# A delta-rule scan before two gated MLPs: the gate made in place in PSUM, second products two steps behind, key operands loaded ahead

## The chip, the cores and the metric

The kernel runs on one core of one Trainium2 chip. The metric is the device time of one execution in microseconds. Of three runs of the kernel before, the median is 1048.21 us (1047.57 to 1048.82).

## The reference

```python
def _attn_ref(q, k, v, beta):
    k_n = k / (norm(k, axis=-1) + 1e-06)
    for t in range(S):
        y[:, :, t] = q[:, :, t] @ state
        v_old = state^T @ k_n[:, :, t]
        state = state + beta[t] * outer(k_n[:, :, t], v[:, :, t] - v_old)
x = y, heads side by side                        # 3072 tokens x 384
h = x @ w_in;  x = (h * sigmoid(1.702 * h)) @ w_out        # first MLP, d_ff 2048
h = max(x @ w_in2, 0);  out = (h * h) @ w_out2             # second MLP, d_ff 2048
```

There are 4 batches, 8 heads, 768 tokens and a head width of 48. All data are float32.

## The kernel before

The scan is cut into 12 chunks of 64 tokens. A chunk `n` goes through `run_a` (keys times keys and keys times queries on PE, copied by ACT into `G` and `pqa`/`pqb`), `solve_in`, `solve_norm`, `solve_prep` and `solve_loop` (a triangular system, on DVE for chunk 0 and on POOL for the others), `finish` and `merge` (transposes and, for chunks 0 to 3, two blocks of 64 small products on PE with an ACT copy into `kT_sb` between them), and then `run_x`, `run_w`, `run_g`, `run_w`, `run_y`, `run_s` (products with the state, whose results are the columns of the MLP's input).

The first MLP (lines 760 to 801, `ph == 1`) takes tiles of 512 tokens, that is two chunks; the second (`ph == 2`) runs after it on the same tiles. One `step` is one of 16 slices of 128 hidden rows. Each float32 operand is split into a high and a low part, so a product is three matmuls (high by high, high by low, low by high). A step puts 9 matmuls of 512 columns into one of two PSUM banks `h`. Then ACT makes tanh (or relu) of the bank into `g`, DVE makes the gated `g` (lines 793 and 796), ACT rounds it into `ghi`, and DVE makes `glo`, the rest. `layer2` adds 9 matmuls with `ghi` and `glo` into three banks `z`. The list `prev` holds steps whose `layer2` is still to come: one for full tiles, two for the half tiles at the start. The first tile is done in halves, since chunk 0 is ready before chunk 1, and while the scan goes on its blocks are put between the steps of the first MLP. The weights are split as they arrive (`split_w`, on ACT, DVE and POOL).

The order on each engine is fixed when the kernel is built. `Program.add` takes an operation with its assumed duration, what it reads and what it writes; `flush` (lines 102 to 187) plays a list schedule with these durations and, on each engine, issues the operation of lowest rank that is ready. On the chip each engine then goes through its list in that order. All DMAs of inputs go out from SP's list.

`load_kq` fetches the operands of `run_a`, four groups of 256 KB for each chunk. From chunk 2 on there are two buffers: groups 0 and 1 are loaded in the scan of two chunks earlier, groups 2 and 3 only behind the products of groups 0 and 1:

```python
put(0, lambda: run_a(m, 0, ((m, 2), (m, 3))))     # line 894
...
mms((1.0, 1.75), todo, reads, [A for _, A in ps_of])   # line 405
for x in nxt:
    load_kq(*x)
```

`run_a` makes, for each pair of groups, 16 products of a 64x64 key block with 128 columns. Only the 32x32 blocks on the diagonal of keys times keys are wanted twice over, so ACT copies each 32-partition strip by itself (lines 412 to 416): two of 256 columns and two of 128 for each group.

## Time and profile before

| | us |
|---|---|
| median of three runs | 1048.21 |
| the profiled execution's own time | 1046.38 |
| its span, first to last instruction | 1044.7 |
| PE busy in the span | 969.3 |
| DVE, ACT, POOL busy | 597.9, 528.4, 336.7 |

PE is TensorE's matmuls, PEld its weight loads, DVE VectorE, ACT ScalarE, POOL GpSimd, SP the queue that issues DMAs. A row of a timeline gives start, duration, engine, line, operation, output and input tiles, count, and in brackets the engine's idle time before it with what ended that. Matmuls overlap in their pipeline, so a single duration is longer than the distance to the next one.

### The profile page before, as it was taken

To read this page: it belongs to the slowest core of one execution; us is meant where nothing else is said; L and a number is where in the kernel's file an instruction comes from. 1 tells how busy PE (TensorE), PEld (TensorE's weight loads), DVE (VectorE), ACT (ScalarE), POOL (GpSimd) and SP (SyncE) were. 2 spreads that over 40 slices of the span, in tenths; PEclk is the share of its full clock that TensorE was granted. 3 is DMA by queue.
4 is the path that set the end of the run, shared out by engine and by line. 5 is a ranking of instruction groups with operands and counts; after the bars stand their busy time and mean duration, and the time that the engine had idled before them with its cause. 6 is when DMAs were issued, how large, how long until landed. Compare 5 with 4: busy or idle time off the path is not lost.

```text
span 1044.7 us, 24071 instructions
## 1 busy us (share of the span) xinstructions
PE 969.3 (93%) x9900; PEld 780.2 (75%) x9900; DVE 597.9 (57%) x1182; ACT 528.4 (51%) x1088; POOL 336.7 (32%) x672
## 2 busy tenths in 40 slices
PE   4479698989888999999999999999999999999998
PEld 3377586767666777777787787788888888888886
DVE  6787786765377576764854667864343333433332
ACT  4566756653655657566535556544343343433333
POOL 2253551288547848748670111210000000000000
PEclk7687888999999999999999999999999999999999
DMA  8254543230322313132111435421010010000000
GB/s 233 85 164 122 168 127 93 65 104 22 96 73 75 97 53 116 43 97 76 55 32 60 137 112 152 121 61 61 1 51 11 0 61 1 21 11 1 31 1 30
DMA packets 43982, 76.33 MB, mean 73 GB/s; under 512 B 6624, under 2 KB 19552, under 8 KB 43872
## 3 DMA queue, kind: packets, MB, share of 16 engines
q1 hardware_dynamic: 43776, 74.75, 23.9%
q8 instruction: 77, 1.26, 0.5%
q14 instruction: 33, 0.27, 0.1%
q10 hardware_dynamic: 96, 0.05, 0.0%
HBM read 64.16 MB, written 9.44 MB: 70 GB/s over the span
## 4 chain that ended last, share of the span: by engine, by line
PE 57%; DVE 16%; POOL 10%; ACT 8%; issue 4%; DMA 3%; SPq 1%; DVEq 0%; ACTq 0%; POOLq 0%
PE z L311 26%; PE h L311 25%; PE a L311 5%; POOL tmpp L567 4%; POOL U L570 4%; ACT G L276 2%; DMA kq<-in_kf 2%; DVE v_sb L286 2%; DVE glo L286 2%; DVE g L293 2%; DVE c L290 1%; DVE c L293 1%; SPq L258 1%; ACT ws L276 1%; ACT ghi L271 1%
## 5 line engine op out<-in xcount | busy, mean ns | idle before, releaser
L271 ACT ACTIVATE g<-h 128x512 f32<-128x512 f32 (+1 forms) x200 | 114.8, 578 | 251.5 <-PE h L311 238.3
L311 PE MATMUL z<-glo,wo_hi 128*128 128x512 f32 (+1 forms) x600 | 232.1, 387 | 8.2 <-DVE glo L286 7.7
L311 PE MATMUL z<-ghi,wo_hi 128*128 128x512 f32 (+1 forms) x600 | 233.4, 389 | 0.1
L311 PE MATMUL z<-ghi,wo_lo 128*128 128x512 f32 (+1 forms) x600 | 230.0, 383 | 0.0
L286 DVE TENSOR_TENSOR glo<-g,ghi 128x512 fp32r<-128x512 f32 (+1 forms) x200 | 140.5, 704 | 100.3 <-ACT ghi L271 98.8
L271 ACT ACTIVATE ghi<-g 128x512 fp32r<-128x512 f32 (+1 forms) x200 | 122.5, 614 | 127.1 <-DVE g L293 64.5
L286 DVE TENSOR_TENSOR g<-g,h 128x512 f32<-128x512 f32 x96 | 66.0, 687 | 157.5 <-ACT g L271 157.5
L311 PE MATMUL h<-x_hi,wi_hi 128*128 128x512 f32 (+1 forms) x312 | 128.1, 411 | 14.4 <-DVE g L293 9.3
L311 PEld LDWEIGHTS z<-glo,wo_hi 128*128 128x128 f32 x600 | 113.8, 190 | 36.7 <-DVE glo L286 15.6
L567 POOL TENSOR_TENSOR tmpp<-U,gu 128x126 f32<-128x126 f32 (+22 forms) x248 | 113.5, 458 | 73.1 <-DVE U L290 54.7
L311 PEld LDWEIGHTS z<-ghi,wo_hi 128*128 128x128 f32 x600 | 113.8, 190 | 23.9 <-ACT ghi L271 0.5
L311 PEld LDWEIGHTS z<-ghi,wo_lo 128*128 128x128 f32 x600 | 113.9, 190 | 21.5
L311 PE MATMUL h<-x_lo,wi_hi 128*128 128x512 f32 (+1 forms) x312 | 120.3, 386 | 0.9 <-DVE x_lo L286 0.8
L311 PE MATMUL h<-x_hi,wi_lo 128*128 128x512 f32 (+1 forms) x312 | 119.5, 383 | 0.0
L570 POOL TENSOR_TENSOR U<-U,tmpp 128x126 f32<-128x126 f32 (+22 forms) x248 | 108.3, 437 | 21.1 <-DVE U L290 2.1
L311 PE MATMUL h<-x_hi,vi_hi 128*128 128x512 f32 x288 | 112.3, 390 | 0.0
L311 PE MATMUL h<-x_hi,vi_lo 128*128 128x512 f32 x288 | 112.1, 389 | 0.0
L293 DVE SCALAR_TENSOR_TENSOR g<-g,h 128x512 f32<-128x512 f32 (+1 forms) x104 | 66.1, 641 | 68.8 <-ACT g L271 68.3
L311 PEld LDWEIGHTS h<-x_hi,wi_hi 128*128 128x128 f32 x312 | 61.0, 195 | 35.5 <-DVE g L293 15.5
L311 PEld LDWEIGHTS h<-x_hi,wi_lo 128*128 128x128 f32 x312 | 61.3, 197 | 11.0
L311 PEld LDWEIGHTS h<-x_lo,wi_hi 128*128 128x128 f32 x312 | 61.4, 197 | 10.0 <-DVE x_lo L286 1.4
L286 POOL TENSOR_TENSOR wo_lo<-c,wo_hi 128x384 fp32r<-128x384 f32 x21 | 22.6, 1075 | 132.4 <-ACT wo_hi L271 132.4
(119 smaller groups left out, 1365.1 us busy)
## 6 DMA issues: line engine op xcount, KB each, us to landing
...
kq<-in_kf SPq DMA_DIRECT2D x44, 256.0 KB, 3.9
...
xf_sb<-zd SPq DMA_DIRECT2D x18, 256.0 KB, 2.7
out<-zs SPq DMA_DIRECT2D x18, 256.0 KB, 2.0
```

The source lines that it names most:

```text
L258: pg.add(queue, 0.07, lambda e: e.dma_start(out=dst, in_=src), reads, writes, early, nbytes)
L271: pg.add("act", c_act(n), lambda e: e.activation(**kw), reads, writes, early)
L276: e.activation(out=out, in_=in_, func=AF.Copy)
L286: pg.add(queue, cost, lambda e: e.tensor_tensor(out=out, in0=in0, in1=in1, op=op), reads, writes, early)
L290: pg.add("dve", c_dve(n, True), lambda e: e.tensor_scalar(**kw), reads, writes, early)
L293: pg.add("dve", c_dve(n), lambda e: e.scalar_tensor_tensor(**kw), reads, writes, early)
L311: e.matmul(out=out, lhsT=lhsT, rhs=rhs, start=start, stop=stop)
L567: e.tensor_tensor(out=t, in0=U[:, lo:hi, j:j + 1].to_broadcast(shape), in1=gu[:, j + 1:, j:j + 1].rearrange("p i o -> p o i").to_broadcast ...
L570: e.tensor_tensor(out=U[:, lo:hi, j + 1:], in0=U[:, lo:hi, j + 1:], in1=t, op=ALU.add)
```

## The change

- `step` writes the gated value over its own `h` bank: DVE's output, ACT's input for `ghi` and DVE's input for `glo` are all that bank. `g` is one buffer of 512 columns in place of two and holds only the tanh or relu. `ghi` and `glo` have three buffers each.
- `layer2` runs two steps behind for all tiles, and what is left is done at the end.
- All four groups of `load_kq` have a buffer from chunk 2 on, and all four are loaded in the scan of two chunks earlier.
- `run_a` makes its products in blocks of 64 rows by 32 columns and puts the second diagonal block where one copy of 128 partitions by 256 columns takes all of `G` of a group. The lower strips skip what is not used, but for chunks 0 and 1, whose banks were never written.
- The buffers `xs` and `tmpd` are gone: `Td` and the second `gu` take their place, so chunk 0's solve on DVE also counts as a writer of the second `gu`.
- Nearly all assumed durations, latencies and DMA rates of the planner have new values, so the order moves on every engine.

```diff
-    LATENCY, OWN_LATENCY = 0.2, 0.12
-    TICK, WARM_COLUMNS = 3.41, 3060
-    DMA_START, DMA_END, DMA_RATE = 1.2, 1.0, 330e3
+    LATENCY, OWN_LATENCY = 0.13, 0.12
+    TICK, WARM_COLUMNS = 3.413, 2950
+    DMA_START, DMA_END, DMA_RATE = 1.6, 0.8, 300e3
...
-    NG = 2
-    g_sb = several(main, "g", NG, [128, TT])
+    NG = 3
+    g_sb = main.tile([128, TT], F32, name="g_sb")
...
-    xs_sb = att.tile([128, CT], F32, name="xs_sb")
+    xs_of = [t.rearrange("p a t -> p (a t)")[:, 0:CT] for t in Td_sb]
...
-        pg.add(queue, 0.07, lambda e: e.dma_start(out=dst, in_=src), reads, writes, early, nbytes)
+        pg.add(queue, 0.62 if nbytes < 40000 else 0.42, lambda e: e.dma_start(out=dst, in_=src), reads, writes, early, nbytes)
...
-            t, keys = kq_sb[g % 2], [("kq", g % 2)]
+            t, keys = (kq_sb, kq1_sb)[g // 2][g % 2], [(("kq", "kq1")[g // 2], g % 2)]
...
-                    o = r if e else 64 - r
-                    todo.append((ps_of[e][0][o:o + 64, 128 * p:128 * p + 128], tiles[e][r:r + 64, 0, p, :], tiles[e][r:r + 64, :, p, :], True, True))
-        mms((1.0, 1.75), todo, reads, [A for _, A in ps_of])
-        for x in nxt:
-            load_kq(*x)
+                    o, t = r if e else 64 - r, tiles[e][r:r + 64, :, p, :]
+                    out = ps_of[e][0][:, 128 * p:128 * p + 128]
+                    todo.append((out[o:o + 32], t[:, 0, 0:32], t, True, True))
+                    low = out[o + 32:o + 64].rearrange("p (c t) -> p c t", c=4)
+                    todo.append((low[:, ::3], t[:, 0, 32:64], t[:, :, 32:64], True, True))
+                    if n < 2:
+                        todo.append((low[:, 1:3], t[:, 0, 32:64], t[:, :, 0:32], True, True))
+        mms((1.25, 2.1), todo, reads, [A for _, A in ps_of])
...
-            for r in range(0, 128, 32):
-                if r % 64 == 0:
-                    copy(256, [A], [("G", i, g + e, r)], G[r:r + 32, sl, :], v4[r:r + 32, :, 0, :])
-                else:
-                    copy(128, [A], [("G", i, g + e, r)], G[r:r + 32, sl, 0:32], v4[r:r + 32, :, 0, 32:64])
+            copy(256, [A], [("G", i, g + e, r) for r in range(0, 128, 32)], G[:, sl, :], v4[:, :, 0, :])
...
-            pg.add(queue, cost, fn, gu_keys(n) + [("U", n % 2)], [("U", n % 2)] + (["first"] if n == 0 and j == 14 else []))
+            pg.add(queue, cost, fn, gu_keys(n) + [("U", n % 2)], [("U", n % 2)] + (gu_keys(1) if queue == "dve" else []) + (["first"] if n == 0 and j == 14 else []))
...
-        g, hi, lo = (x[s][:, o:o + n] for x in (g_sb, ghi_sb, glo_sb))
-        kg, khi, klo = ([(x, s, i) for i in parts] for x in ("g", "ghi", "glo"))
+        g, hi, lo = g_sb[:, o:o + n], ghi_sb[s][:, o:o + n], glo_sb[s][:, o:o + n]
+        kg = [("g", i) for i in parts]
+        khi, klo = ([(x, s, i) for i in parts] for x in ("ghi", "glo"))
         if ph == 1:
             act(n, [("h", p)], kg, out=g, in_=ps, func=AF.Tanh, scale=GATE / 2)
-            stt(n, [("h", p)] + kg, kg, out=g, in0=g, scalar=1.0, in1=ps, op0=ALU.add, op1=ALU.mult)
+            stt(n, [("h", p)] + kg, [("h", p)], out=ps, in0=g, scalar=1.0, in1=ps, op0=ALU.add, op1=ALU.mult)
         else:
             act(n, [("h", p)], kg, out=g, in_=ps, func=AF.Relu)
-            tt(n, [("h", p)] + kg, kg, g, g, ps, ALU.mult)
-        act(n, kg, khi, out=hi, in_=g)
-        tt(n, kg + khi, klo, lo, g, hi, ALU.subtract)
+            tt(n, [("h", p)] + kg, [("h", p)], ps, g, ps, ALU.mult)
+        act(n, [("h", p)], khi, out=hi, in_=ps)
+        tt(n, [("h", p)] + khi, klo, lo, ps, hi, ALU.subtract)
         prev.append((ph, j, f, c0, n, hi, lo, khi + klo))
-        while len(prev) > (1 if n == TT else TUNE["depth"]):
+        while len(prev) > TUNE["depth"]:
             layer2(*prev.pop(0))
...
-                put(4, lambda: load_kq(m + 2, 0), lambda: load_kq(m + 2, 1), lambda: load_q(m + 2))
+                put(4, *[lambda g=g: load_kq(m + 2, g) for g in range(4)], lambda: load_q(m + 2))
...
-            put(0, lambda: run_a(m, 0, ((m, 2), (m, 3))))
+            put(0, lambda: run_a(m, 0))
...
-        layer2(*prev.pop(0))
+        while prev:
+            layer2(*prev.pop(0))
```

The order at three places follows. The first is ACT at chunk 0's merge: the copy that the second block of the merge waits for is `kT_sb<-a_72`. Before:

```order
L276 ACTIVATE G_106<-z_69 32x4x32
L276 ACTIVATE G_106<-z_69 32x256
L276 ACTIVATE G_106<-z_69 32x4x32
L276 ACTIVATE G_106<-z_70 32x256
L276 ACTIVATE G_106<-z_70 32x4x32
L276 ACTIVATE G_106<-z_70 32x256
L276 ACTIVATE G_106<-z_70 32x4x32
L276 ACTIVATE G_106<-z_71 32x256
L276 ACTIVATE G_106<-z_71 32x4x32
L276 ACTIVATE G_106<-z_71 32x256
L276 ACTIVATE G_106<-z_71 32x4x32
L276 ACTIVATE kT_sb<-a_72 128x256
```

With the change:

```order
L277 ACTIVATE G_107<-a_74 128x256
L277 ACTIVATE G_107<-z_69 128x256
L272 ACTIVATE wi_hi<-c_93 128x384
L272 ACTIVATE c_92<-raw_90 128x384
L277 ACTIVATE G_107<-z_70 128x256
L277 ACTIVATE G_107<-z_71 128x256
L277 ACTIVATE pqa_103<-a_74 64x256
L277 ACTIVATE kT_sb<-a_72 128x256
L272 ACTIVATE wo_hi<-c_94 128x384
L272 ACTIVATE c_92<-raw_91 128x384
```

The 16 narrow copies of `G` for chunk 1 (12 of them below `z`, four of another bank ahead of these rows) become four, one weight split stands between them, and the copy into `kT_sb` follows after one copy of `pqa`.

The second is PE in the second MLP. Here `h_67` and `h_68` are the two banks of the step, `z_69` to `z_71` the three output banks. Before:

```order
L311 MATMUL h_68<-x_hi_80,vi_hi 128x512
L311 MATMUL h_68<-x_lo_81,vi_hi 128x512
L311 MATMUL h_68<-x_hi_80,vi_lo 128x512
L311 MATMUL h_67<-x_hi_80,vi_hi 128x512
L311 MATMUL h_67<-x_lo_81,vi_hi 128x512
L311 MATMUL h_67<-x_hi_80,vi_lo 128x512
L311 MATMUL h_68<-x_hi_80,vi_hi 128x512
L311 MATMUL h_68<-x_lo_81,vi_hi 128x512
L311 MATMUL h_68<-x_hi_80,vi_lo 128x512
L311 MATMUL z_69<-ghi_84,wo_hi 128x512
L311 MATMUL z_69<-glo_86,wo_hi 128x512
L311 MATMUL z_69<-ghi_84,wo_lo 128x512
```

With the change:

```order
L313 MATMUL h_68<-x_hi_80,vi_hi 128x512
L313 MATMUL h_68<-x_lo_81,vi_hi 128x512
L313 MATMUL h_68<-x_hi_80,vi_lo 128x512
L313 MATMUL z_69<-ghi_84,wo_hi 128x512
L313 MATMUL z_69<-glo_87,wo_hi 128x512
L313 MATMUL z_69<-ghi_84,wo_lo 128x512
L313 MATMUL h_68<-x_hi_80,vi_hi 128x512
L313 MATMUL h_68<-x_lo_81,vi_hi 128x512
L313 MATMUL h_68<-x_hi_80,vi_lo 128x512
L313 MATMUL z_70<-ghi_84,wo_hi 128x512
L313 MATMUL z_70<-glo_87,wo_hi 128x512
L313 MATMUL z_70<-ghi_84,wo_lo 128x512
```

Before, nine matmuls of `h` are followed by nine of `z`; now they alternate in threes, and so it goes on for the rest of the second MLP.

The third is SP behind chunk 1's output, where the operands for chunk 3 are loaded (`raw` is weights). Before:

```order
L258 DMA k_sb<-in_kt 128x768
L258 DMA raw_89<-in_w_out 128x768
L258 DMA kq_99<-in_kf 128x512
L258 DMA kq_100<-in_kf 128x512
L258 DMA raw_90<-in_w_in 128x768
L258 DMA raw_88<-in_w_out 128x768
L258 DMA kq_99<-in_kf 128x512
L258 DMA kq_100<-in_kf 128x512
L258 DMA raw_89<-in_w_in 128x768
L258 DMA raw_90<-in_w_out 128x768
L258 DMA raw_88<-in_w_in 128x768
L258 DMA kT_sb<-in_kq 128x4x256
```

With the change:

```order
L259 DMA xf_sb<-Td_113 16x256 x6
L259 DMA pqa_103<-in_kq 64x4x256
L259 DMA pqb_105<-in_kq 64x4x256
L259 DMA raw_91<-in_w_in 128x768
L259 DMA k_sb<-in_kt 128x768
L259 DMA raw_89<-in_w_out 128x768
L259 DMA kq_100<-in_kf 128x512
L259 DMA kq_101<-in_kf 128x512
L259 DMA kq_98<-in_kf 128x512
L259 DMA kq_99<-in_kf 128x512
L259 DMA raw_90<-in_w_in 128x768
```

Four loads of `kq` in a row, into four buffers, stand in place of two and, three rows on, two more into the same two buffers.

## Rows read from the trace of the kernel before

**Rows 1.** the page, parts 1 and 6: busy time; loads, KB each, median us to landing.
```profile
PE 969.3 (93%) x9900; PEld 780.2 (75%) x9900; DVE 597.9 (57%) x1182; ACT 528.4 (51%) x1088; POOL 336.7 (32%) x672
...
kq<-in_kf SPq DMA_DIRECT2D x44, 256.0 KB, 3.9
```

**Rows 2.** busy time by engine in four stretches (then PEclk, DMA share, GB/s).
```profile
0.00:60.00 60.00, 28.40 (x732) 22.35 (x732) 44.86 (x143) 31.81 (x79) 18.03 (x30) 0.68 0.58 164
60.00:200.00 140.00, 121.62 (x2395) 102.47 (x2396) 107.28 (x236) 89.74 (x218) 52.69 (x104) 0.86 0.41 123
200.00:600.00 400.00, 379.04 (x4843) 293.55 (x4842) 246.13 (x484) 230.31 (x487) 243.59 (x519) 1.00 0.25 75
600.00:1045.00 445.00, 440.20 (x1934) 361.88 (x1932) 199.60 (x321) 176.58 (x307) 22.34 (x21) 1.00 0.14 43
```

**Rows 3.** who PE waited for, 60 to 600 us: total us, times, longest.
```profile
PE a L311 <- DMA kq<-in_kf: 9.7, 9, 3.5
PE h L311 <- DVE g L293: 9.3, 10, 1.8
PE z L311 <- DVE glo L286: 7.0, 9, 2.0
```

**Rows 4.** timeline of ACT, 6 to 42 us (start, us, idle before).
```profile
9.48 2.65 ACT L276 ACTIVATE G<-z 32x256 f32<-32x256 f32 x8
...
30.95 0.52 ACT L271 ACTIVATE wo_hi<-c 128x384 fp32r<-128x384 f32 x1 [5.79 <-DVE c L293]
...
32.83 3.98 ACT L276 ACTIVATE G<-z 32x256 f32<-32x256 f32 x12
36.83 0.38 ACT L276 ACTIVATE kT_sb<-a 128x256 f32<-128x256 f32 x1
```

**Rows 5.** timeline of DVE, 9 to 16 us.
```profile
9.63 0.38 DVE L290 TENSOR_SCALAR U<-sm_s,dup_sb 128x16 f32<-128x16 f32 x2
13.33 0.65 DVE L290 TENSOR_SCALAR c<-raw 128x384 uint16<-128x384 uint16 x2 [3.32 <-DMA raw<-in_w_in]
13.87 1.90 DVE L296 STREAM_TRANSPOSE gu<-G 128x1024 f32<-128x1024 f32 x1
```

**Rows 6.** timeline of PE: start-up, two later waits, two warm blocks.
```profile
27.55 1.05 PE L311 MATMUL z<-g 64*64 64x128 f32 x32
...
37.27 2.01 PE L311 MATMUL a<-kT_sb 16*32 16x16 f32 x128 [7.48 <-ACT kT_sb L276]
40.53 1.50 PE L311 MATMUL a<-v_sb,Td 32*32 32x48 f32 x64 [1.25 <-DVE Td L286]
...
60.56 0.58 PE L311 MATMUL h<-x_hi,wi_hi 128*128 128x256 f32 x1 [2.13 <-ACT x_hi L271]
...
115.87 2.65 PE L311 MATMUL a<-kq 64*64 64x128 f32 x32 [3.52 <-DMA kq<-in_kf]
...
444.05 1.10 PE L311 MATMUL a<-kq 64*64 64x128 f32 x32
...
467.36 0.88 PE L311 MATMUL a<-v_sb,Td 32*32 32x48 f32 x64
```

**Rows 7.** groups of instructions by line and form: count, busy us, mean ns.
```profile
L286 DVE TENSOR_TENSOR glo<-g,ghi 128x512 fp32r<-128x512 f32 x184 | 132.1, 719 | 98.6 <-ACT ghi L271 97.0
...
L293 DVE SCALAR_TENSOR_TENSOR g<-g,h 128x512 f32<-128x512 f32 x88 | 59.5, 682 | 67.1 <-ACT g L271 66.7
...
L276 ACT ACTIVATE G<-a 32x256 f32<-32x256 f32 x86 | 32.1, 373 | 11.2 <-PE a L311 10.0
...
L276 ACT ACTIVATE G<-a 32x128 f32<-32x128 f32 x86 | 23.1, 269 | 1.0
...
L271 ACT ACTIVATE g<-h 128x256 f32<-128x256 f32 x16 | 5.9, 378 | 6.2 <-PE h L311 6.0
```

**Rows 8.** timeline of ACT and DVE in the last step.
```profile
1036.12 0.60 ACT L271 ACTIVATE g<-h 128x512 f32<-128x512 f32 x1 [1.41 <-PE h L311]
...
1038.14 0.69 DVE L286 TENSOR_TENSOR glo<-g,ghi 128x512 fp32r<-128x512 f32 x1 [0.70 <-ACT ghi L271]
```

More of the change, by code (lines that the diff above doesn't have):

```diff
@@ L252, with c_act, c_dve @@
     v_sb = att.tile([128, NP, D], F32, name="v_sb")
-    xs_sb = att.tile([128, CT], F32, name="xs_sb")
+    xs_of = [t.rearrange("p a t -> p (a t)")[:, 0:CT] for t in Td_sb]
     sm = {x: att.tile([128, 32], F32, name=f"sm_{x}") for x in ("bt", "y", "a", "b", "s", "nu", "s2")}
-    tmp_sb = {"pool": [att.tile([128, 136], F32, name="tmpp")], "dve": several(att, "tmpd", 2, [128, 84])}
+    tmp_sb = {"pool": [att.tile([128, 136], F32, name="tmpp")], "dve": [gu_sb[1][:, 128 * i:128 * i + 128] for i in range(2)]}
     def dma(dst, src, reads, writes, nbytes, early=0, queue="sp"):
-        pg.add(queue, 0.07, lambda e: e.dma_start(out=dst, in_=src), reads, writes, early, nbytes)
-    def c_act(n):
-        return 0.08 + 0.00083 * n
-    def c_dve(n, fast=False):
-        return 0.07 + (0.00052 if fast else 0.00104) * n
+        pg.add(queue, 0.62 if nbytes < 40000 else 0.42, lambda e: e.dma_start(out=dst, in_=src), reads, writes, early, nbytes)
+    def c_act(n, part=128):
+        return 0.1 + 0.00079 * n if part == 128 else 0.165 + 0.00087 * n
+    def c_dve(n, fast=False, part=128):
+        return 0.07 + (0.00052 if fast else 0.00104) * n + (0.09 if part < 128 and n > 64 else 0.0)
     def c_pool(n):
-        return 0.22 + 0.0021 * n
+        return 0.25 + 0.0022 * n
     def act(n, reads, writes, early=0, **kw):
         kw.setdefault("func", AF.Copy)
-        pg.add("act", c_act(n), lambda e: e.activation(**kw), reads, writes, early)
+        pg.add("act", c_act(n, kw["out"].shape[0]), lambda e: e.activation(**kw), reads, writes, early)
     def copy(n, reads, writes, out, in_, queue="act", fast=False, early=0):
@@ L278, in fn @@
                 e.tensor_copy(out=out, in_=in_)
-        cost = {"act": c_act(n), "dve": c_dve(n, fast), "pool": c_pool(n)}
+        part = out.shape[0]
+        cost = {"act": c_act(n, part), "dve": c_dve(n, fast, part), "pool": c_pool(n)}
         queue = (queue,) if isinstance(queue, str) else queue
@@ L283, in tt @@
     def tt(n, reads, writes, out, in0, in1, op, queue="dve", early=0):
-        cost = {"dve": c_dve(n), "pool": c_pool(n)}
+        cost = {"dve": c_dve(n, False, out.shape[0]), "pool": c_pool(n)}
         cost = cost[queue] if isinstance(queue, str) else tuple(cost[q] for q in queue)
@@ L300, in tr_parts @@
         if n < 4:
-            tr(1024, reads, writes, out, in_)
+            tr(1740, reads, writes, out, in_)
             return
@@ L342, with bank @@
         [(t, ("h", i)) for i, t in enumerate(h_ps)]
-    def bank(n=3):
+    def bank(n=5 - NH):
         na[0] = (na[0] + 1) % n
@@ L385, in load_kq, with run_a @@
         else:
-            t, keys = kq_sb[g % 2], [("kq", g % 2)]
+            t, keys = (kq_sb, kq1_sb)[g // 2][g % 2], [(("kq", "kq1")[g // 2], g % 2)]
         dma(t, kf[n, g], [], keys, 128 * 8 * C * 4)
         kq_of[n, g] = t, keys
-    def run_a(n, g, nxt=()):
+    def run_a(n, g):
         i, G = n % 2, G_sb[n % 2]
-        ps_of = [bank(8 if n < 2 else 3) for _ in range(2)]
+        ps_of = [bank(8 if n < 2 else 5 - NH) for _ in range(2)]
         todo, reads = [], ["first"] if n == 1 else []
@@ L611, in merge @@
         ps = ps[:, 0:256].rearrange("p (a i) -> p a i", a=NP)
[L612 removed]
+        mms((1.35, 2.1), [(ps[r:r + 32, a, :], Uj[r:r + 16, :, a], Rs[r:r + 16, a, :], True, True) for a, r in tiles],
             KT, [A], 0.1)
@@ L862 @@
         load_q(2)
-        load_kq(2, 0)
-        load_kq(2, 1)
+        for g in range(4):
+            load_kq(2, g)
         load_v(1)
```

42 lines of the change are left out of this document (21 added, 21 removed).

## Prediction, made before the changed kernel was run

> **What bounds the kernel now.** I read the page's busy times first: PE is busy for 969.3 of 1044.7 us [rows 1]. Then the stretches [rows 2]. From 600 us on PE is busy 440.20 of 445 us, and 440.20 us over 1934 matmuls is 0.228 us each, so a step of 18 full matmuls takes 4.1 us. Only removing matmuls could shorten that part, and the change removes none. From 200 to 600 us PE is idle for 21.0 us, from 60 to 200 us for 18.4 us and at a mean granted clock of 0.86, in the first 60 us for 31.6 us. So all that can be won lies ahead of 600 us. For 60 to 600 us the waits of PE say what it lacked [rows 3]: operands of `run_a` 9.7 us, an `h` bank not yet read by line 293 9.3 us, a `glo` not yet made 7.0 us. For the first 60 us I read three timelines: ACT [rows 4], DVE [rows 5] and PE [rows 6]. The reader should see there that the first MLP starts at 60.56 us, at the end of a chain through chunk 0's merge in which PE waits 7.48 us for one ACT copy.
>
> **Start-up: -9.6 us.** DVE has finished the inputs of chunk 0's solve at 9.63 + 0.38 = 10.01 us, but next in its list stands a weight split whose load lands only at 13.33 us; the transpose of `G` starts at 13.87 [rows 5]. In the new order the transpose comes first. `G` itself must be there: before, its second eight copies ran from 9.48 to 12.13 us [rows 4]; now four copies of 128x256 do the whole chunk. No row shows that copy of `G`, but tanh of the same shape from PSUM takes 378 ns, against 2 x 373 + 2 x 269 = 1284 ns for the four strips [rows 7]. Two of them follow PE's second pair of groups, so `G` is ready before 10 us and the solve starts 3.9 us earlier. On ACT the second piece comes out. There a rounding of weights waits 5.79 us, and the sixteen copies of chunk 1's `G` stand between it and the copy to `kT_sb`, which starts at 36.83 [rows 4]. The products for these copies begin to end at 27.55 [rows 6], now 3.9 us earlier, 23.6. Ahead of the `kT_sb` copy the new list of ACT has four copies of `G` (4 x 0.378), one rounding (0.52), one weight copy and one of `pqa` (0.4 to 0.55 each): 3.0 us, and I allow 0.6 us for the rounding's input. That gives 27.2 in place of 36.83, which is 9.6 us earlier. The merge's second block (37.27), `run_w` (40.53) and the first step (60.56) [rows 6] hang on that copy one behind the other. Ends: 3.9 us if only the first piece comes, 12 us if DVE's norms, which follow chunk 1's `G`, also get out of the way.
>
> **Operands ahead: -9.7 us, and -1.5 us of clock.** Groups 2 and 3 of a chunk were asked for only when groups 0 and 1 had been used. Now all four go out some three steps before use, at least 12 us, and a load of 256 KB lands 3.9 us after issue in the median [rows 1]. So nine waits of 9.7 us in all [rows 3] should go. SP's list has the third and fourth load wait for the last use of their buffers, one chunk back; behind them stand loads of weights, but that use lies five steps earlier, so I cost it at nothing (if it came late, weights would be late next). Behind the longest wait, 3.52 us, the block of products took 2.65 us, against 1.10 us for the same rows at full clock [rows 6]; I count the 1.5 us. Ends: 5 and 13 us.
>
> **In place, two steps behind: -8 us.** `layer2` of a step now comes a whole step later, so a late `glo` no longer stops PE while the older one is there to be worked on. On the other side the bank is held until `glo` is made. In the last step the chain from tanh's start to `glo`'s end is 1036.12 to 1038.83, 2.7 us [rows 8]; until line 293 or 296 it would be half of that. In the new order, h and z alternate in threes, and between the end of a step's `h` and the next use of its bank stand seven threes, 7 x 3 x 0.228 = 4.8 us. Undisturbed, 2.1 us are left over, so the second MLP loses nothing. In 200 to 600 us DVE is busy for 246 and ACT for 230 of 400 us [rows 2], and the four instructions queue behind the scan's. Of 9.3 + 7.0 us [rows 3] I take half as won: the second kind goes, the first stays. Ends: 0 and 16 us. DVE and ACT change little: `glo` from two SBUF operands takes 719 ns, line 293 with one operand from PSUM 682 ns [rows 7], so reading the bank is no dearer here. A new wait is that tanh needs the single `g` free, and ACT's list stands behind it. Line 293 of the step before has read `g` long before, unless two banks end together, as the half tiles do; the two halves of `g` are for that.
>
> **64x32 blocks: +3 us.** For each of 20 `run_a` from chunk 2 on, PE gets 32 products in place of 16, each of two passes, with 128 or 64 columns: in columns, 1.5 times as much. If four blocks run at a time, as with 64x64, 1.10 us [rows 6] becomes 1.65; if eight do, the rate of issue decides, and 64 short matmuls of `run_w` took 0.88 us [rows 6]. So -0.2 to +0.55 us each, -4 to +11 us in all; no row shows eight at a time, and I take +0.15 us, 3 us. ACT loses 1284 - 378 = 0.9 us per group, 3.6 us per chunk, beside PE's work; I count that only as part of the 8 us above.
>
> The Trainium skill, "TensorEngine Tiling (Array Packing)", Performance Considerations, Instruction Overhead, speaks against this: some 60 cycles for each matmul however short, which is 25 ns at full clock. By it, 64 matmuls would need 1.6 us and the term would be an estimated +10 us, the forecast 7 us longer. The trace does not agree for small blocks: the 64 of `run_w` took 0.88 us [rows 6], 14 ns each.
>
> Everything else I cost at nothing. `xs` in `Td` and `tmpd` in the second `gu` are free when they are needed: chunk 1's products already waited for the end of chunk 0's solve. The end of the kernel has one more `layer2` to cover the last `glo`, some tenths of a microsecond.
>
> **Sum.** -9.6 - 9.7 - 1.5 - 8 + 3 = -25.8 us. The profiled execution would go from 1046.38 to 1020.6 us; it lies 1.8 us under the median of the runs shown, so for the median I forecast 1048.2 - 25.8 = **1022.4 us**. A measurement of this kernel can tell about 0.2%, 2.1 us, from no change.
>
> **Rivals.**
>
> 1. *The head start is eaten.* Between 60 and 200 us DVE is busy 107 of 140 us and ACT 90 [rows 2] with weight splits and with chunks 1 and 2, and POOL's solve of chunk 1 stands in the way of the second half tile. If these don't move forward with the first step, PE starts sooner and waits later. For: DVE at 77%. Against: chunk 1's `G` comes as much earlier as chunk 0's merge, and ACT has less to do. Time: 1022.4 + 9.6 = 1032.0 us; with the blocks at their upper end, 1040.
> 2. *The slow clock goes too.* PE is busy for 121.6 us between 60 and 200 us at a clock of 0.86 [rows 2], where the two levels are 1.2 and 2.4 GHz. The lost 14% are 17 us. If a list with fewer waits keeps the clock up for half of it, 1022.4 - 8.5 = 1013.9 us; for all of it, 1005.4. For: the row at 115.87 shows the slow clock right behind a wait. Against: much of that stretch is small products, which wait for DVE and ACT still.
> 3. *The bank is held too long, slower.* Holding a bank through `ghi` and `glo` adds 1.4 us to each step. With DVE and ACT 60% busy in 200 to 600 us, the chain of 2.7 us can grow beyond 4.8 us plus what the scan puts between. There are 88 full steps in the first MLP [rows 7]; this decides against the change from 25.8 / 88 = 0.3 us a step on. At half of the added hold, 0.7 us a step, it costs 62 us: 1084 us. Against: the lists are built knowing it, `z` work of the step before is there, and ACT's load falls. The Trainium skill, "Perfetto Trace Analysis", Optimizing Scalar/DVE Operations, has DVE's access cost at about 125 ns in PSUM against 60 in SBUF, which would hold each bank an estimated 0.13 us longer; the 682 and 719 ns above do not agree with that for reads, and no row shows DVE writing to PSUM.
> 4. *Nothing comes of it.* The loads land as late as before because SP is late, and the new order loses elsewhere what it gains at the start: 1046 to 1050 us.
>
> **How the numbers follow.** The forecast as it stands (1014 to 1030) gets 0.46, rival 1 0.24, rival 2 0.20, rival 3 0.06, rival 4 0.04, of which half lies within 0.2%. The range reaches from rival 2 at its full size, 1005, to rival 1 with the dearer blocks, 1040, and leaves out rivals 3 and 4. Faster by over 0.2%: 0.46 + 0.24 + 0.20 + 0.01 = 0.91; within 0.2% 0.02; slower 0.06 + 0.01 = 0.07.
>
> **What would show it.** In the new profile the first matmul of `h` should start at 50 to 52 us; no wait of PE for `kq` should be left after the start but tenths; a block of `run_a` should last 0.9 to 1.65 us at full clock; waits of `h` for `glo` should appear in place of those for line 293, under 10 us together; from 600 us on nothing should move. The prediction is wrong if the first step starts early and PE's idle time between 60 and 200 us grows by as much, or if waits for `glo` pass 25 us.

## The result, and the profile after

The changed kernel takes **1015.86 us** in the median of four runs (1015.43 to 1018.74); the kernel before took 1047.89 us beside it. The ratio is 0.970, with a 95% interval of 0.968 to 0.972. The forecast was 1022.4 us, with a range of 1005 to 1040. The sum was 25.8 us; 32.0 us were gained. As will be seen, the total came out near because misses of its terms partly cancel.

The page of the kernel after, its busy times, its instruction queue (packets, megabytes, share of the 16 DMA engines) and one of its loads; the first line answers to [rows 1]:

```profile
PE 961.4 (95%) x10796; PEld 784.9 (77%) x10796; DVE 594.8 (59%) x1194; ACT 471.3 (46%) x944; POOL 311.1 (31%) x660
...
q8 instruction: 84, 1.38, 0.6%
...
kq<-in_kf SPq DMA_DIRECT2D x44, 256.0 KB, 4.0
```

The four stretches, as in [rows 2]:

```profile
0.00:60.00 60.00, 35.35 (x1002) 28.63 (x1003) 44.09 (x141) 25.06 (x59) 21.84 (x40) 0.69 0.65 184
60.00:200.00 140.00, 121.69 (x2763) 104.06 (x2762) 115.44 (x253) 81.12 (x191) 57.12 (x110) 0.85 0.43 126
200.00:600.00 400.00, 394.20 (x5226) 313.05 (x5226) 256.99 (x516) 206.73 (x420) 222.71 (x503) 1.00 0.26 79
600.00:1014.00 414.00, 410.15 (x1809) 339.17 (x1807) 178.33 (x286) 158.34 (x277) 9.41 (x9) 1.00 0.13 39
```

PE's idle time fell from 31.6 to 24.65 us in the first 60, from 18.4 to 18.3 us between 60 and 200, and from 21.0 to 5.8 us between 200 and 600. Add the 7.9 us by which PE is busy for less, and 30.2 of the 30.9 us between the two spans are accounted for: half of it lies between 200 and 600 us, while the forecast had put 9.6 of 25.8 us into the start. POOL is busy for 222.71 us there where it was 243.59. A third of that is 16 of the solve's products, which now come ahead of 200 us; the rest is shorter products, and the change does nothing to them. The page has them, before and then after:

```profile
L567 POOL TENSOR_TENSOR tmpp<-U,gu 128x126 f32<-128x126 f32 (+22 forms) x248 | 113.5, 458 | 73.1 <-DVE U L290 54.7
...
L570 POOL TENSOR_TENSOR U<-U,tmpp 128x126 f32<-128x126 f32 (+22 forms) x248 | 108.3, 437 | 21.1 <-DVE U L290 2.1
```

```profile
L568 POOL TENSOR_TENSOR tmpp<-U,gu 128x126 f32<-128x126 f32 (+22 forms) x248 | 108.0, 435 | 73.4 <-DVE U L292 55.2
...
L571 POOL TENSOR_TENSOR U<-U,tmpp 128x126 f32<-128x126 f32 (+22 forms) x248 | 99.1, 400 | 22.2 <-DVE U L292 3.1
```

From 458 to 435 and from 437 to 400 ns: that is the first sign of what the forecast had missed.

Who PE waited for between 60 and 600 us, as in [rows 3]:

```profile
PE a L313 <- DVE Td L288: 7.8, 6, 2.1
PE h L313 <- DVE glo L288: 6.8, 9, 2.6
PE a L313 <- DVE ws L288: 2.4, 2, 2.0
...
PE z L313 <- DVE glo L288: 1.7, 1, 1.7
```

No wait for `kq` is left. The wait of `h` for line 293 has become one for `glo`, 6.8 us, and that of `z` for `glo` has nearly gone. These signs came as the forecast named them. The largest wait now is that for the solve's result `Td`, 7.8 us. In the kernel before it was small:

```profile
PE a L311 <- DVE Td L286: 3.2, 2, 3.0
```

Of the three timelines that follow, that of DVE answers to [rows 5], that of ACT to [rows 4] and that of PE to [rows 6]:

```profile
9.81 1.93 DVE L298 STREAM_TRANSPOSE gu<-G 128x1024 f32<-128x1024 f32 x1
```

```profile
30.52 0.38 ACT L277 ACTIVATE kT_sb<-a 128x256 f32<-128x256 f32 x1 [2.61 <-PE a L313]
```

```profile
29.41 1.05 PE L313 MATMUL a<-Td,G 32*32 32x16 f32 x63 [2.63 <-issue]
...
56.11 0.39 PE L313 MATMUL h<-x_hi,wi_hi 128*128 128x256 f32 x1 [2.84 <-ACT x_hi L272]
...
332.91 1.14 PE L313 MATMUL a<-kq 64*32 64x128 f32 x64
```

The transpose starts at 9.81 us (10.0 was forecast), the copy to `kT_sb` at 30.52 (27.2), the first MLP at 56.11 (50 to 52, and 60.56 before). A block of `run_a` takes 1.14 us.

The groups, as in [rows 7]:

```profile
L288 DVE TENSOR_TENSOR glo<-h,ghi 128x512 fp32r<-128x512 f32 x184 | 126.7, 689 | 79.3 <-ACT ghi L272 76.9 <-PE z L313 1.1
...
L295 DVE SCALAR_TENSOR_TENSOR h<-g_sb,h 128x512 f32<-128x512 f32 x88 | 61.1, 695 | 62.2 <-ACT g_sb L272 61.4
```

In the mean `glo` is 30 ns shorter with `h` from the bank, and line 295, which writes to one, is 13 ns longer. The 30 ns are not the price of the operand: where POOL is idle, `glo` takes 691 ns before (132 of them) and 690 after (128); where POOL works beside it, 789 (52) and 686 (56).

### The profile page after: what moved, and what is told of

Its sections match the earlier page's. It is cut to its first block, busy times and chain, and to the rows that moved or that the text cites. A ratio compares the mean times of both kernels' runs of the same rounds, so it can differ in the third digit from the quotient of the medians.

```text
span 1013.8 us, 25665 instructions
## 1 busy us (share of the span) xinstructions
PE 961.4 (95%) x10796; PEld 784.9 (77%) x10796; DVE 594.8 (59%) x1194; ACT 471.3 (46%) x944; POOL 311.1 (31%) x660
## 3 DMA queue, kind: packets, MB, share of 16 engines
q8 instruction: 84, 1.38, 0.6%
## 4 chain that ended last, share of the span: by engine, by line
PE 66%; DVE 12%; POOL 11%; ACT 4%; issue 4%; DMA 2%; SPq 0%; POOLq 0%; ACTq 0%; DVEq 0%
PE h L313 30%; PE z L313 30%; PE a L313 6%; POOL tmpp L568 4%; POOL U L571 4%; DVE v_sb L288 2%; DVE h L295 2%; POOL tmpp L538 1%; DVE glo L288 1%; POOL U L540 1%; DVE kT_sb L306 1%; DVE c L292 1%; DVE kT_sb L298 1%; DMA pqa<-in_kq 1%; PE a L509 1%
## 5 line engine op out<-in xcount | busy, mean ns | idle before, releaser
L272 ACT ACTIVATE g_sb<-h 128x512 f32<-128x512 f32 (+1 forms) x200 | 115.8, 579 | 275.6 <-PE h L313 274.1
L272 ACT ACTIVATE ghi<-h 128x512 fp32r<-128x512 f32 (+1 forms) x200 | 116.0, 580 | 139.3 <-DVE h L295 81.8
L288 DVE TENSOR_TENSOR glo<-h,ghi 128x512 fp32r<-128x512 f32 (+1 forms) x200 | 133.2, 666 | 79.4 <-ACT ghi L272 76.9
L288 DVE TENSOR_TENSOR h<-g_sb,h 128x512 f32<-128x512 f32 x96 | 66.8, 696 | 171.5 <-ACT g_sb L272 171.5
L568 POOL TENSOR_TENSOR tmpp<-U,gu 128x126 f32<-128x126 f32 (+22 forms) x248 | 108.0, 435 | 73.4 <-DVE U L292 55.2
L295 DVE SCALAR_TENSOR_TENSOR h<-g_sb,h 128x512 f32<-128x512 f32 (+1 forms) x104 | 68.0, 653 | 67.0 <-ACT g_sb L272 66.1
L571 POOL TENSOR_TENSOR U<-U,tmpp 128x126 f32<-128x126 f32 (+22 forms) x248 | 99.1, 400 | 22.2 <-DVE U L292 3.1
L313 PEld LDWEIGHTS h<-x_hi,vi_hi 128*128 128x128 f32 x288 | 54.1, 188 | 11.3
```

What stands on the lines that cost most here:

```text
L272: pg.add("act", c_act(n, kw["out"].shape[0]), lambda e: e.activation(**kw), reads, writes, early)
L288: pg.add(queue, cost, lambda e: e.tensor_tensor(out=out, in0=in0, in1=in1, op=op), reads, writes, early)
L295: pg.add("dve", c_dve(n), lambda e: e.scalar_tensor_tensor(**kw), reads, writes, early)
L313: e.matmul(out=out, lhsT=lhsT, rhs=rhs, start=start, stop=stop)
L568: e.tensor_tensor(out=t, in0=U[:, lo:hi, j:j + 1].to_broadcast(shape), in1=gu[:, j + 1:, j:j + 1].rearrange("p i o -> p o i").to_broadcast ...
L571: e.tensor_tensor(out=U[:, lo:hi, j + 1:], in0=U[:, lo:hi, j + 1:], in1=t, op=ALU.add)
```

## Experiments

Unless it says otherwise, an experiment is the changed kernel with one part undone, so its time is read against 1015.9 us. Each was timed beside the kernel before, and the ratios are to that one. The list is planned anew for each.

### Operands asked for late again (no_ahead)

```diff
-            t, keys = (kq_sb, kq1_sb)[g // 2][g % 2], [(("kq", "kq1")[g // 2], g % 2)]
+            t, keys = kq_sb[g % 2], [("kq", g % 2)]
...
-            put(0, lambda: run_a(m, 0))
+            put(0, lambda: run_a(m, 0, ((m, 2), (m, 3))))
```

> The changed kernel (1015.9 us), but operands of groups 2 and 3 of a chunk are asked for only when groups 0 and 1 have been used, in the same two buffers. Theory (the term of the prediction): waits of PE for kq of 8 to 12 us come back between 60 and 600 us, and the time is 11 us longer, 1027 us (1022 to 1031). Rival (the new durations let the list put other work before the products, so that little is lost): kq waits under 4 us, 1016 to 1020 us.

Measured: 1023.78 us, ratio 0.977 (0.975 to 0.979), so **the early loads are worth 7.9 us**. But the waits that the theory named are not what is lost: `kq` is waited for 0.6 us in all. The stretches show part of where it went:

```profile
60.00:200.00 140.00, 121.60 (x2613) 105.68 (x2614) 110.31 (x245) 77.38 (x182) 50.79 (x95) 0.81 0.40 121
200.00:600.00 400.00, 390.17 (x5336) 307.85 (x5332) 253.53 (x503) 205.29 (x418) 226.60 (x519) 1.00 0.26 80
```

Between 200 and 600 us PE is idle for 4.0 us more than in the kernel after. Between 60 and 200 us its clock is 0.81 where it was 0.85, which over 140 us is worth 5.6 us, but this cannot be put down to the loads: the profiled execution is the slowest of four (1026.23 us), the mean granted clock of those four is 0.954 to 0.963, and of the four of the kernel after 0.954 to 0.961. The theory had the size, the rival had the waits: a list that knows that the operands are late works around them. Where it pays for the rest of the 7.9 us stays open.

### One step behind, gate in its bank (one_behind)

```diff
-        while len(prev) > TUNE["depth"]:
+        while len(prev) > (1 if n == TT else TUNE["depth"]):
```

> The changed kernel, but the second matrix's products of a full step come one step behind, as before; the gate stays in its bank. Theory (the term of the prediction): waits of z for glo of about 7 us come back between 60 and 600 us, 1023 us (1019 to 1027). Rival A: the bank, held longer and with nothing else to work on, stops PE for much more, over 20 us: above 1036 us. Rival B: making it in place carries the gain and the step of distance nothing: 1015 to 1018 us.

Measured: 1043.84 us, ratio 0.996 (0.994 to 0.997): nearly the whole gain is gone, 28.0 us. Rival A is right in size and wrong in how it looks: waits of `z` for `glo` are 7.4 us between 60 and 600 us, and 0.7 us after that. Most of the loss lies behind that: from the last copy of `z` of tile 4 (at 564.1 us here, 556.4 after) to that of the last tile (1037.2 and 1010.2) it is 19 us, and PE shows hardly any idle time there. It stands in the groups of PE between 640 and 1000 us. First this kernel, then the kernel after:

```profile
L313 PE MATMUL z<-glo,wo_hi 128*128 128x512 f32 x255 | 107.0, 419 | 0.0
L313 PE MATMUL h<-x_hi,vi_hi 128*128 128x512 f32 x257 | 100.3, 390 | 0.0
```

```profile
L313 PE MATMUL z<-glo,wo_hi 128*128 128x512 f32 x265 | 103.2, 389 | 0.0
```

And in the timeline of one step, PE and then DVE:

```profile
801.12 0.39 PE L313 MATMUL z<-ghi,wo_hi 128*128 128x512 f32 x1
801.37 0.50 PE L313 MATMUL z<-glo,wo_hi 128*128 128x512 f32 x1
801.71 0.40 PE L313 MATMUL z<-ghi,wo_lo 128*128 128x512 f32 x1
```

```profile
800.62 0.69 DVE L288 TENSOR_TENSOR glo<-h,ghi 128x512 fp32r<-128x512 f32 x1 [0.67 <-ACT ghi L272]
```

`glo` is finished at 801.31 us. The first matmul that reads it is written down as 0.50 us long, and the next starts 0.34 us after it, not 0.23. A short wait of PE is booked as a longer matmul, not as idle. This happens once in each step, and with some hundredths around it a tile of 16 steps in the second MLP takes 67.9 us in place of 65.3, 0.16 us a step. So rival 3 of the forecast, the bank held too long, is a real mechanism at a distance of one: to find its bank free, the list puts `z` sooner behind its own `h` (2.7 us of PE's work between them, counted in the list, where the kernel before has 4.1), and `glo` is just not there. With the gate in SBUF at the same distance (gate_sbuf_one, next) the same group takes 390 ns.

### Gate back in SBUF, and how far behind (gate_sbuf, gate_sbuf_one, hold_list, gate_sbuf_three)

```diff
-    g_sb = main.tile([128, TT], F32, name="g_sb")
+    g_sb = several(main, "g", 2, [128, TT])
-    glo_sb = several(main, "glo", NG, [128, TT], F32R)
+    glo_sb = several(main, "glo", 2, [128, TT], F32R)
...
-            stt(n, [("h", p)] + kg, [("h", p)], out=ps, in0=g, scalar=1.0, in1=ps, op0=ALU.add, op1=ALU.mult)
+            stt(n, [("h", p)] + kg, kg, out=g, in0=g, scalar=1.0, in1=ps, op0=ALU.add, op1=ALU.mult)
...
-        act(n, [("h", p)], khi, out=hi, in_=ps)
-        tt(n, [("h", p)] + khi, klo, lo, ps, hi, ALU.subtract)
+        act(n, kg, khi, out=hi, in_=g)
+        tt(n, kg + khi, klo, lo, g, hi, ALU.subtract)
```

> The changed kernel, still two steps behind, but the gate is made in one of two SBUF tiles, so that the bank is free after line 295 or 298 (glo has two buffers in place of three, for the space). Theory (the longer hold costs what the trace of the changed kernel shows as waits of h for glo): those waits, 6.8 us between 60 and 600 us, go, and the time is 1009 to 1013 us. Rival A: at two steps behind the hold is free, since the waits turn up elsewhere: 1014 to 1018 us. Rival B: the second buffer of glo is missed: over 1019 us.

> The same with full steps one behind, as before the change: of the change only the operands ahead, the 64x32 blocks and the durations are left. Theory (in place and two behind together are worth the 8 us of the prediction): 1024 us (1019 to 1030), with waits of z for glo and of h for the bank of 10 us or more between 60 and 600 us. Rival: the loss of the kernel with the gate in its bank and one behind (1043.8 us) comes only from the held bank, so this one lies at 1015 to 1018 us, 65.3 us per tile in the second MLP, and the pair is worth nothing by itself.

Measured: gate_sbuf 1049.55 us, ratio 1.001 (1.000 to 1.002); gate_sbuf_one, which adds the edit of one_behind, 1041.01 us, ratio 0.993 (0.991 to 0.995). Both expectations for gate_sbuf_one (1019 to 1030 us, 1015 to 1018) are missed. Against this run, which has the MLP of the kernel before, **in place and two behind together are worth 25.2 us**, three times the term of the forecast. gate_sbuf came out as its rival B (over 1019 us), and it answers another question than the one it was made for. With two buffers of `glo`, a step has written its `glo` into the buffer of the step two before by the time that the products of that one are issued: the second matrix's products then take `ghi` of their own step and `glo` of a newer one (this part of the computation is changed in it and in hold_list), and a distance of two waits on the newest `glo`. A distance needs as many buffers and one more.

```diff
-        act(n, kg, khi, out=hi, in_=g)
-        tt(n, kg + khi, klo, lo, g, hi, ALU.subtract)
+        act(n, [("h", p)] + kg, khi, out=hi, in_=g)
+        tt(n, [("h", p)] + kg + khi, klo, lo, g, hi, ALU.subtract)
```

> The kernel with the gate in SBUF, two steps behind (1049.6 us), with one edit: the list is told that a bank is held until glo is made, as it is with the gate in place. The bank on the chip is still free after line 295. In the list's order the work of PE between the end of an h and the next use of its bank grows from a median of 3.3 to 6.1 us in the first MLP (counted as in the kernels with the gate in place, which have 5.0). Theory (in place gains because it makes the list use a bank later, so that a late line 295 no longer stops PE): most of the 34 us come back, 1015 to 1025 us, with waits of h for g under 4 us where there were 11.0. Rival (in place gains by what it does on the chip, fewer or faster SBUF accesses, or the missing third buffer of glo is what costs): 1040 us or more.

Measured: 1121.65 us, ratio 1.071 (1.068 to 1.073). The time is in the rival's range (1040 us or more), but far beyond gate_sbuf's, and for the missing buffer: it is the same flaw, now with a bank that the list gives out late. It waits on the newest `glo` again and again, between 60 and 600 us and from 600 on:

```profile
PE z L313 <- DVE glo L288: 24.0, 27, 2.6
```

```profile
PE z L313 <- DVE glo L288: 35.9, 52, 1.6
```

So it does not test the theory. The last run mends the flaw: three buffers of `glo` and of `ghi`, two of `g`, the room for them taken from the early loads. It stands beside no_ahead.

```diff
-    kq1_sb = several(att, "kq1", 2, [128, 2, 4, C])
+    kq1_sb = several(att, "kq1", 1, [128, 2, 4, C])
...
-    g_sb = main.tile([128, TT], F32, name="g_sb")
+    g_sb = several(main, "g", 2, [128, TT])
```

> Gate in SBUF, two steps behind, and this time three buffers of glo, so that the products two steps behind find their own glo; the room comes from loading operands as late as before, so this one stands beside the kernel without the early loads (1023.8 us), from which it differs only in where the gate is made. Theory (a distance of two steps with a buffer for each is what pays, and making the gate in place does no more than free the room for the third buffers): 1019 to 1028 us. Rival (the bank given back late is itself what keeps the list from running PE into line 295): 1035 us or more, with waits of h for g of 8 us or more between 60 and 600 us.

Measured: 1037.21 us, ratio 0.991 (0.989 to 0.993), 13.4 us over no_ahead. Both explanations fail. The theory's 1019 to 1028 us is missed, so in place does more than free room; the rival has the time (1035 us or more), but its waits for line 295 are 2.0 us, not 8. What has grown is the wait for the solve's result, in the first row (gate_sbuf_three) from the second (no_ahead):

```profile
PE a L313 <- DVE Td L288: 13.9, 9, 4.7
```

```profile
PE a L313 <- DVE Td L288: 5.0, 4, 2.1
```

That is 8.9 us. The two profiled executions lie 9.4 us apart (1035.63 and 1026.23), and PE's idle time between 200 and 600 us is 18.6 against 9.8 us; what makes up the 13.4 us between the medians beyond that is not shown. The two lists differ too, but other lists of one kernel (old_plan, merge_cost) lie within 2 us of it. The solve is POOL's, so its groups come next, of gate_sbuf_three and then of no_ahead:

```profile
L570 POOL TENSOR_TENSOR tmpp<-U,gu 128x126 f32<-128x126 f32 (+22 forms) x248 | 116.3, 469 | 67.6 <-DVE U L292 49.2
L573 POOL TENSOR_TENSOR U<-U,tmpp 128x126 f32<-128x126 f32 (+22 forms) x248 | 109.5, 442 | 20.4 <-DVE U L292 1.1
```

```profile
L570 POOL TENSOR_TENSOR tmpp<-U,gu 128x126 f32<-128x126 f32 (+22 forms) x248 | 105.4, 425 | 76.3 <-DVE U L292 57.8
L573 POOL TENSOR_TENSOR U<-U,tmpp 128x126 f32<-128x126 f32 (+22 forms) x248 | 98.7, 398 | 20.3 <-DVE U L292 1.0
```

The same 496 instructions take 44 ns more each where the gate is in SBUF. The timeline shows which ones. In the kernel before, POOL and then DVE around 342 us:

```profile
342.00 0.37 POOL L567 TENSOR_TENSOR tmpp<-U,gu 128x81 f32<-128x81 f32 x1
342.45 0.34 POOL L570 TENSOR_TENSOR U<-U,tmpp 128x81 f32<-128x81 f32 x1
342.86 0.36 POOL L567 TENSOR_TENSOR tmpp<-U,gu 128x78 f32<-128x78 f32 x1
343.30 0.66 POOL L570 TENSOR_TENSOR U<-U,tmpp 128x78 f32<-128x78 f32 x1
```

```profile
341.70 0.69 DVE L293 SCALAR_TENSOR_TENSOR g<-g,h 128x512 f32<-128x512 f32 x1
343.08 0.69 DVE L286 TENSOR_TENSOR glo<-g,ghi 128x512 fp32r<-128x512 f32 x1 [0.70 <-ACT ghi L271]
```

And in the kernel after, again POOL and then DVE:

```profile
485.54 0.37 POOL L568 TENSOR_TENSOR tmpp<-U,gu 128x78 f32<-128x78 f32 x1
485.99 0.33 POOL L571 TENSOR_TENSOR U<-U,tmpp 128x78 f32<-128x78 f32 x1
```

```profile
485.35 0.69 DVE L288 TENSOR_TENSOR glo<-h,ghi 128x512 fp32r<-128x512 f32 x1
```

In the kernel before, the product that starts at 343.30, behind a `glo` that runs until 343.77, takes 0.66 us; its neighbour of nearly the same size takes 0.34, and the one at 342.00, beside line 293, which has one operand in a bank, 0.37. In the kernel after, two products beside a `glo` take 0.37 and 0.33 us. Counted over all of the solve's products between 60 and 600 us, against the same form with DVE idle: those that overlap a `glo` are longer by some 170 ns (47 of `tmpp`) and 260 ns (44 of `U`) in the kernel before, by 224 and 207 ns in gate_sbuf_three, by 15 and 9 ns (64 and 57) in the kernel after. Those that in the kernel before overlap nothing but the making of the gate, which has one operand in a bank, are longer by 1 and 2 ns (32 and 30). POOL is held up while DVE subtracts two SBUF operands, and with the gate in its bank `glo` has only one.

### Old blocks for chunks 0 and 1 (old_blocks_start)

```diff
+                    if n < 2:
+                        o = r if e else 64 - r
+                        todo.append((ps_of[e][0][o:o + 64, 128 * p:128 * p + 128], tiles[e][r:r + 64, 0, p, :], tiles[e][r:r + 64, :, p, :], True, True))
+                    else:
...
```

> The changed kernel, but chunks 0 and 1 are multiplied in 64x64 blocks and copied in strips as before (16 matmuls for each pair of groups where there are 48); later chunks keep 64x32. Theory: the two gaps of 2.6 and 1.2 us inside the blocks of the merge, which the trace puts down to issue, come from the 192 short matmuls ahead of them and go; the copy to kT_sb starts about 2 us earlier in spite of the strips and the first MLP at 53 to 54 us. Rival: the gaps have another cause and stay; the strips then put the first MLP at 57 us or later. Whether a start moved by 3 us carries to the end: 1013 us if it does, 1015 to 1017 if tile 0 ends no earlier.

Measured: 1020.52 us, ratio 0.973 (0.971 to 0.976), 4.7 us over the kernel after, whose ratio's interval (0.968 to 0.972) just touches this one, and above both times named. The gaps put down to issue are gone, as the theory has it, but the strips of `G` on ACT (16 copies for chunk 1, as in [rows 4]) keep the copy to `kT_sb` until 33.46 us and PE waits 5.4 us for it. The first MLP starts at 55.21 us all the same, 0.9 us earlier than after, and still the median is higher: PE is idle for 27.1 of the first 60 us, 2.4 us more, and for 1.3 us more up to 200 us. When the first step starts is not a full measure of the start; the idle time ahead of 200 us tells more.

### Fewer matmuls at the start (start_two)

```diff
-                    todo.append((out[o:o + 32], t[:, 0, 0:32], t, True, True))
                     low = out[o + 32:o + 64].rearrange("p (c t) -> p c t", c=4)
+                    if n < 2:
+                        todo.append((out[o:o + 64], t[:, 0, :], t, True, True))
+                    else:
+                        todo.append((out[o:o + 32], t[:, 0, 0:32], t, True, True))
...
```

> The changed kernel, but in chunks 0 and 1 a pair of blocks takes two matmuls in place of three (one of 64x64, then the lower 64x32 over it): 128 matmuls for the two chunks where there were 192. Theory (the gaps put down to issue are PE waiting for its instructions, so they shrink with their number): the gap of 2.6 us in the merge's first block falls below 2 us and the copy to kT_sb comes 0.5 to 2 us earlier; the first MLP hardly moves, 55 to 56 us, because DVE with chunk 1's norms is late next; 1014 to 1017 us. Rival: the gap stays at 2.6 us.

Measured: 1063.99 us, ratio 1.015 (1.012 to 1.017), slower by 48.1 us. Chunk 0's blocks, of which 84 matmuls take 1.38 us in the kernel after (16 ns each), crawl here:

```profile
6.54 12.84 PE L313 MATMUL a<-kq 64*64 64x128 f32 x56 [0.76 <-DMA kq<-in_kf]
```

That is 0.23 us a matmul. Two things differ: large and small tiles alternate, and the small one writes rows that the large one has just written. No run tells them apart. In the merge the gap of 2.63 us is gone and that of 1.20 is 0.49 us, as the theory has it; but behind products this slow the instructions would have had time to arrive in any case, so it is no test of their number. One thing is clean: the first MLP starts at 104.49 us, 48.4 us late, and the kernel ends 48.1 us late. Of a delay at the start nothing is made good.

### The old durations (old_plan)

```diff
-    LATENCY, OWN_LATENCY = 0.13, 0.12
-    TICK, WARM_COLUMNS = 3.413, 2950
-    DMA_START, DMA_END, DMA_RATE = 1.6, 0.8, 300e3
+    LATENCY, OWN_LATENCY = 0.2, 0.12
+    TICK, WARM_COLUMNS = 3.41, 3060
+    DMA_START, DMA_END, DMA_RATE = 1.2, 1.0, 330e3
...
```

(and all costs of single instructions with them)

> The changed kernel, but the list is planned with the durations, latencies and DMA figures of the kernel before. Theory (the prediction costed them at nothing): 1012 to 1020 us, the scatter of lists. Rival: the durations are what places the work rightly, and a good part of the gain is theirs: 1026 us or more, with idle time of PE between 60 and 600 us over 10 us longer.

Measured: 1016.41 us, ratio 0.971 (0.969 to 0.973). The new durations are worth 0.5 us, nothing that can be measured. The list is a different one (waits of `h` for `glo` are 15.1 us where they were 6.8, and the clock between 60 and 200 us is 0.91), and the time is the same: two lists can lose the same time in different places.

### Three candidates (merge_cost, nh3, nh3_merge)

```diff
-        mms((1.35, 2.1), [(ps[r:r + 32, a, :], G[r:r + 32, a, 0:32], Td[r:r + 32, a, 16:32], True, True) for a, r in tiles],
+        mms((3.9, 4.7) if n == 0 else (1.35, 2.1), [(ps[r:r + 32, a, :], G[r:r + 32, a, 0:32], Td[r:r + 32, a, 16:32], True, True) for a, r in tiles],
...
-        mms((1.35, 2.1), [(ps[r:r + 32, a, :], Uj[r:r + 16, :, a], Rs[r:r + 16, a, :], True, True) for a, r in tiles],
+        mms((2.5, 3.3) if n == 0 else (1.35, 2.1), [(ps[r:r + 32, a, :], Uj[r:r + 16, :, a], Rs[r:r + 16, a, :], True, True) for a, r in tiles],
```

> The changed kernel; in the list alone, chunk 0's two merge blocks are planned at 3.9 and 2.5 us in place of 1.35 each, which is what they took with the gaps put down to issue. Theory (DVE is late next at the start because the list, not knowing the gaps, put chunk 1's norms ahead of chunk 0's subtraction): the wait of PE for v_sb, 3.6 us, falls below 1.5 us and the first MLP starts at 52 to 54.5 us in place of 56.1; 1012 to 1015 us. Rival: the norms have to be done anyway and the first MLP stays at 56 us, or the head start is gone by the end of tile 0: 1015 to 1017 us.

```diff
-    NH = 2
+    NH = 3
```

> The changed kernel with three h banks and two a banks in place of two and three. Theory (the attention's products come in pairs of banks, and with two banks each pair waits until ACT and DVE have emptied the one before): waits of a for ACT and DVE grow by over 10 us, 1025 to 1045 us. Rival: the waits of h for glo go (6.8 us) and the attention hardly misses the bank, as PE works on the MLP meanwhile: 1009 to 1014 us.

> Three h banks and the dearer merge blocks together, as a candidate for a better kernel. Theory (the two add up): 1009 to 1012 us. Rival (the list scatters by more than either is worth): 1012 to 1017 us.

Measured: merge_cost 1014.08 us, ratio 0.967 (0.965 to 0.969); nh3 1012.74, ratio 0.966 (0.963 to 0.969); both together 1013.41, ratio 0.966 (0.964 to 0.968). All three medians lie 2 to 3 us under the changed kernel's, and all intervals overlap with its own; they do not add up. With merge_cost the wait for `v_sb` falls from 3.6 to 2.0 us and the first MLP starts at 55.0 us, short of the theory's 54.5. With three `h` banks the waits of `h` for `glo` are gone and the attention does not miss its bank, against the theory; but other waits fill their place, so that PE is idle for 5.9 us between 200 and 600 us where it was 5.8.

## Why the prediction came out as it did

**Start-up, -9.6 us: mis-sized; the first step came 4.5 us earlier.** Taking back the wide copies and the small blocks of chunks 0 and 1 (old_blocks_start) costs 4.7 us. The first piece is right to 0.2 us (the transpose). The step that failed is the sum over ACT's list, "27.2 in place of 36.83", where 30.52 was measured: it took PE's block ahead of the `kT_sb` copy to run through. PE stopped inside it for 2.63 us, and for 1.20 us inside the next one, both put down to issue. The page gives a likely cause. 84 packets in the instruction queue for 10796 matmuls and as many weight loads are 257 instructions a packet, and 77 packets for 9900 before are 257 too, and in the trace both gaps end 1.2 to 1.3 us after a packet of this queue has landed. Chunk 1's blocks, right ahead of the merge, are 192 matmuls with 64x32 tiles (two passes for each of 96 products) where the kernel before has 64 with 64x64, and the merge's two blocks are 128 each. That the gaps are waits for instructions is argued, not shown; that they go with the 64x32 blocks of the start is what old_blocks_start shows. The other loss is a DVE that is late with chunk 1's norms, so that PE waits 3.60 us for `v_sb`. The rows of DVE, and then of POOL:

```profile
38.23 0.21 DVE L295 SCALAR_TENSOR_TENSOR sm_b<-sm_a,gu 128x32 f32<-128x32 f32 x1
38.37 0.38 DVE L292 TENSOR_SCALAR c<-raw 128x384 uint16<-128x384 uint16 x1
38.64 1.15 DVE L295 SCALAR_TENSOR_TENSOR sm_y<-sm_b,sm_y 128x32 f32<-128x32 f32 x1
...
40.17 1.12 DVE L288 TENSOR_TENSOR sm_a<-sm_y 128x32 f32<-128x32 f32 x1
```

```profile
38.44 1.30 POOL L428 TENSOR_SCALAR_AFFINE_SELECT pqa<-pqa 64x1024 f32<-64x1024 f32 x1 [1.38 <-ACT pqa L277]
39.81 1.45 POOL L428 TENSOR_SCALAR_AFFINE_SELECT pqb<-pqb 64x1024 f32<-64x1024 f32 x1
```

A norm of 128x32 takes 0.2 us and here 1.15 and 1.12: each ends within 0.05 us of the instruction of POOL that was under way. It is the hold-up of the solve's products seen from the other side, as are the 789 ns of a `glo` beside POOL.

**Operands ahead, -9.7 and -1.5 us: 7.9 us measured.** All waits for `kq` went, as forecast. The clock of 60 to 200 us did not rise (0.86 to 0.85), so the second term is not seen. The order of size is right, and the account of it by single waits is not: with the loads late again only 0.6 us of such waits came back.

**In place, two steps behind, -8 us: the failed step.** Measured as a pair it is 25.2 us. "Of 9.3 + 7.0 us I take half as won" priced only the waits of PE that bear the names of the MLP, and "DVE and ACT change little" priced `glo` by its own 719 ns. The first is near enough for the distance alone: one step behind, with the gate in SBUF (gate_sbuf_one) PE waits 10.5 us for line 295 and 9.4 for `glo` and `ghi`, two steps behind (gate_sbuf_three) 2.0 and 3.2. Whom a `glo` with two SBUF operands keeps waiting was never asked, although POOL is busy beside it for 243.59 of the 400 us [rows 2]. The waits of the kernel before could not price it: PE waited 3.2 us for the solve's result, and the solve became the next limit only when the other waits were gone. The Trainium skill, "SBUF — State Buffer", section "SBUF: two separate sides", says that DVE and POOL share a pair of ports, and that of an operation of DVE with two SBUF inputs and one of POOL that reads SBUF, whichever starts first has the pair for its whole length while the other blocks fully. The trace agrees that both are held up: 170 to 260 ns for each solve product that meets a `glo` before, 9 to 15 ns after, and some 100 ns for each `glo` that meets POOL before, none after. In place needs the distance, but not the other way round. In place without the distance is 1043.8 us, 2.8 us slower than neither (1041.0). The distance without in place was run without the early loads only, at 1037.2 us; if their 7.9 us may be taken off, an estimate, it is 1029.3 us, 11.7 us faster than neither, and in place adds the 13.4 us of the last run.

**64x32 blocks, +3 us: +0.8 us on PE.** A block takes 1.14 us against 1.10 before [rows 6], so 20 x 0.04. That is 18 ns a matmul. The rule weighed in the forecast, of the Trainium skill, "TensorEngine Tiling (Array Packing)", Performance Considerations, Instruction Overhead, by which 64 would have taken an estimated 1.6 us, is not borne out by this row either. What the number of matmuls did cost came, it seems, at the start, as above. No run takes the blocks of chunk 2 and later back, so what the wider copies spare ACT there (471.3 us busy in all, 528.4 before) is not priced.

**Costed at nothing.** The durations are worth 0.5 us. From 600 us on nothing moved: PE is busy for 410.15 of 414 us, over 1809 matmuls 0.227 us each, as before.

**Sum and rivals.** The forecast was 6.2 us too small. By terms, the pair was given 17.2 us too little, the start up to 5.1 and the operands 3.3 too much, and the blocks 2.2 of cost too much: 17.2 - 5.1 - 3.3 + 2.2 = 11.0 us. The 4.8 us between that and 6.2 are what parts that are undone one at a time do not add up to: gate_sbuf_one, which has the change without the pair, lies only 7.6 us under the kernel before beside it, where the other terms make 11.6. So the nearness of the total is luck in part: the largest term is missed by a factor of three, and too much at the start and for the operands makes up for half of it. The head start was not eaten between 60 and 200 us (rival 1: idle time 18.4 to 18.3 us), and the clock did not rise (rival 2). Rival 3 is seen in one_behind, at a distance of one only, and there it costs 2.8 us against the gate in SBUF. Rival 4, that nothing comes of it, is out.
